# Tap and bias rows spread by TensorE, two whole filter transforms, wide FIR matmuls and DMA transposes in an SSM convolution with an MLP

## The chip, the cores and the metric

The kernel runs on one core of a Trainium2 chip. The metric is the device time of one execution in microseconds. The engines are PE (TensorE, matmuls, with weight loads shown apart as PEld), DVE (VectorE), ACT (ScalarE), POOL (GpSimd) and SP (SyncE, which issues DMAs). Data lies in SBUF; PE writes to PSUM, and DVE or ACT move results from there ("eviction").

## The reference

Two layers of two parts each, on a sequence of 2048 rows with 512 channels, all in bf16:

```python
def _A_ref(q, k, v, shift_k, ssm_k, ssm_D):          # q is the normed x
    for t in range(4):
        k_shift = k_shift + k_pad[:, t:t + S, :] * shift_k[:, 3 - t]
    kv = k_shift * v
    y = irfft(rfft(kv padded to 2S) * rfft(ssm_k padded to 2S))[:S]   # long causal convolution
    y = y + kv * ssm_D
    return q * y

def _B_ref(x, w1, b1, w2, b2):                        # x is normed, and normed again inside
    h = _gelu(_layernorm(x) @ w1 + b1)                # 512 -> 1376
    return h @ w2 + b2                                # 1376 -> 512

x = A_q
for layer in (0, 1):
    x = x + _A_ref(_layernorm(x), A_k, A_v, A_shift_k, A_ssm_k, A_ssm_D)
    x = x + _B_ref(_layernorm(x), B_w1, B_b1, B_w2, B_b2)
```

The convolution's input `kv` and its filter don't depend on x, so its result is computed once and used by both layers.

## The kernel before

**Blocks.** The sequence is cut into four blocks of 512 rows, b = 0 to 3, and so is the filter. Each block of 512 rows is transformed with 1024-point tables, as matmuls. `forward` transforms a block: for two sets of frequencies c and for the even and odd rows it runs 4 matmuls of 512 columns into PSUM, evicts the result, and then adds and subtracts the even and odd halves on DVE (`tt`); that makes 16 matmuls and 4 evictions a block. `spectrum_h(m)` transposes filter block m on PE (16 transposes), evicts it and calls `forward`; the results are called H0 to H3. `shift(b)` is the four-tap filter on k (the FIR): 16 transposes, an eviction, 64 matmuls of 128 x 128 against diagonal matrices that hold the taps, and a product with v. `products(b)` multiplies spectra, the sums over earlier blocks being made by accumulating DMAs from POOL's queue. `wrap(m)` folds filter block m-1 into m. `inverse(b)` transforms back with 16 matmuls.

**The MLP.** `mlp(b, L)` works on one block in layer L: statistics (DVE, with the power of -1/2 on POOL), norms (ACT, `norm`), a product with the convolution's result and an add (DVE), statistics and norms again, 8 PE transposes and an eviction for each pair of 128-row tiles, then 44 matmuls with W1 (11 groups of 4; twice 44 of half the width where PARTS splits the block, as for block 3 in both layers), GELU on ACT with the bias of each group as a per-partition scalar, and 44 matmuls with W2 of 512 columns. The eight MLPs are (block, layer): (0,0), (1,0), (0,1), (2,0), (1,1), (3,0), (2,1), (3,1), about in this order on PE.

**The order of work.** All operations are recorded first, as numbered operations with what they read and write. Three tables then settle where they run: ORDER, one list of all operation numbers, gives each engine's program order; SIDE names those that run on the second of two possible engines; BANKS gives PSUM banks. `replay` goes through the list with assumed durations, `keep_busy` puts dummy matmuls (L913 before, L985 after) into long gaps of PE in that replay, and `sync` adds semaphore waits for what remains dependent. Every engine runs its list strictly in order, so an instruction that waits holds up those behind it. SP's list is the queue of loads, and of the stores.

**The start.** SP loads k's first block, the identity, the taps (pieces of four values, straight into 128 partitions) and the first filter block, in this order. DVE multiplies identity and taps into 16 diagonals in one operation (L570). The MLP bias comes later in the same queue, in two DMAs of two-byte pieces, and POOL casts it to f32 (L549).

**Lines.** L557 is `tt`; L563 and L564 are evictions by ACT and DVE; L575 is a transform matmul; L605 and L629 are the transposes of the filter and of k; L648 is the FIR; L657 is its product with v from PSUM; L738 is the power on POOL; L750 and L752 are statistics; L779 is a norm; L807 is the MLP's transposes; L824 and L843 are W1 and W2; L829 is GELU; L848 and L851 add W2's result to x.

Of the kernel before, what the change touches and what calls it, by code (L numbers as in the profile page):

```python
# [7 lines left out]
ALU = mybir.AluOpType  # L8
# [358 lines left out]
def _tables():  # L367

    t = np.arange(4)[:, None] + 4 * np.arange(128)[None, :]
    kk = np.arange(2)[:, None] + 2 * np.arange(128)[None, :]  # L370
    th = TWO_PI * t[:, :, None, None] * (kk + 0.5) / 1024
    F = np.stack([np.cos(th), -np.sin(th)], 3)
    return F.transpose(1, 0, 2, 3, 4).reshape(128, 2048), F.transpose(4, 2, 3, 0, 1).reshape(128, 2048) / 512


SIDE = [30, 204, 508, 590, 728, 750, 831, 912, 933]
BANKS = "020402242404224400262556463010456340262616542032024240042240042440066016553462243501654013266102613202040404062341663552015021261526103315215340424444026015654624643030521242141654360010665123404156021610322554431541243501601"
ORDER = [
# [44 lines left out]
U = 512  # L423


def bass_interleave_layers__ssm_conv_h3__mixer_channel_mlp__prompt_kernel(
# [120 lines left out]
    for p0, n, o, c in ((0, 128, 0, 10), (0, 96, 10, 1)):  # L547
        d, s = M(p0, n, M_B1 + o, [1, c]), A(p0, n, R_B1 + o // 10 * 16, [1, c])
        P.op(POOL, lambda e, d=d, s=s: e.tensor_copy(d, s), 300.0, reads=[s], writes=[d])  # L549
# [394 lines left out]
```

## Time and profile before

| | us |
|---|---|
| median of 3 runs | 245.52 (245.1 to 245.62) |
| the profiled execution | 244.91 |
| its span, first to last instruction | 243.1 |
| PE busy | 232.9 (96%) |
| DVE busy | 185.1 (76%) |
| ACT busy | 181.6 (75%) |
| POOL busy | 68.0 (28%) |

The profile is of one execution. A row of the timeline gives start, length, engine, line, operation, output and input, and the count of instructions merged into it; in brackets stands the idle time ahead of it and what ended it. The chain of waits follows the last instruction back from releaser to releaser. A busy PE is not PE at its peak, since matmuls are pipelined and their recorded lengths overlap: what a stream of matmuls costs is the distance from one to the next.

### The profile page before, as it was taken

Reading aid. Unit: us, or ns where it says so; the run is one execution under the profiler, and the core shown is the slowest. Engines: PE = TensorE matmul, PEld = TensorE weight load, DVE = VectorE, ACT = ScalarE, POOL = GpSimd, SP = SyncE. Lnnn points to the kernel's source line nnn. Section 1 sums busy time; section 2 is a strip of 40 time slices with the busy share of each in tenths; the row PEclk is TensorE's granted clock in tenths of the full one; section 3 lists DMA queues with packets and bytes.
Section 4 is the critical chain, followed back from the end, with each engine's and each line's share of the span. In section 5 each row is a group of like instructions: output and inputs, shape, how many; then the busy total and the mean of one; then the engine's idle time right before and its main releaser. Section 6 shows DMA issues by size and latency. Waiting matters only on the chain.

```text
span 243.1 us, 3962 instructions
## 1 busy us (share of the span) xinstructions
PE 232.9 (96%) x1551; PEld 131.9 (54%) x1574; DVE 185.1 (76%) x357; ACT 181.6 (75%) x279; POOL 68.0 (28%) x73
## 2 busy tenths in 40 slices
PE   8999996989999999999999999999999999999994
PEld 3756632647655684445444544544468654448841
DVE  1379999999999999999999999783977242574004
ACT  2358998999899589979799285579968657955730
POOL 0000134432572356753146315241310201120000
PEclk9999999999999999999999999999999999999999
DMA  6999916668794099990089989920002000002002
GB/s 189 392 377 220 391 52 238 105 242 162 142 158 62 0 173 173 175 174 3 0 162 185 172 215 226 207 47 3 1 0 89 0 0 3 0 0 86 3 0 86
DMA packets 14406, 29.85 MB, mean 123 GB/s; under 512 B 3026, under 2 KB 8500, under 8 KB 14260
## 3 DMA queue, kind: packets, MB, share of 16 engines
q0 software_dynamic: 5232, 15.21, 32.9%
q1 hardware_dynamic: 9156, 14.40, 17.2%
q8 instruction: 12, 0.20, 0.3%
q14 instruction: 6, 0.05, 0.1%
HBM read 12.30 MB, written 2.10 MB: 59 GB/s over the span
## 4 chain that ended last, share of the span: by engine, by line
PE 67%; DVE 22%; issue 5%; ACT 3%; POOL 2%; DVEq 0%; POOLq 0%
PE ps L824 28%; PE ps L843 26%; DVE ar L557 14%; PE ps L575 6%; DVE sm L750 4%; PE ps L913 3%; PE ps L807 2%; POOL sm L738 2%; ACT ar L779 1%; DVE ar L657 1%; ACT ar L563 1%; DVE ar L851 1%; PE ps L629 1%; PE ps L648 1%; DVE sm L752 1%
## 5 line engine op out<-in xcount | busy, mean ns | idle before, releaser
L557 DVE TENSOR_TENSOR ar<-ar 128x2048 bf16<-128x2048 bf16 (+2 forms) x125 | 115.1, 954 | 9.3 <-ACT ar L563 4.8
L824 PE MATMUL ps<-ar 128*128 128x256 bf16 (+3 forms) x479 | 80.2, 320 | 1.2 <-ACT ar L563 0.9
L563 ACT ACTIVATE ar<-ps 128x1024 bf16<-128x1024 f32 (+2 forms) x61 | 64.3, 1115 | 22.0 <-PE ps L575 10.3
L843 PE MATMUL ps<-ar 128*128 128x512 bf16 (+1 forms) x339 | 79.6, 379 | 0.7
L829 ACT ACTIVATE ar<-ps,sm 128x256 bf16<-128x256 f32 (+3 forms) x121 | 61.5, 572 | 16.5 <-PE ps L824 16.2
L738 POOL TENSOR_TENSOR sm<-sm 128x2 f32<-128x2 f32 x32 | 39.0, 1218 | 104.6 <-DVE sm L757 45.1
L824 PEld LDWEIGHTS ps<-ar 128*128 128x128 bf16 (+1 forms) x484 | 47.7, 100 | 32.3 <-ACT ar L563 1.8
L779 ACT ACTIVATE ar<-ar,sm 128x512 bf16<-128x512 bf16 x64 | 48.4, 808 | 13.3 <-DVE sm L739 13.1
L843 PEld LDWEIGHTS ps<-ar 128*128 128x128 bf16 (+1 forms) x352 | 34.1, 98 | 37.0 <-ACT ar L829 1.2
L575 PE MATMUL ps<-ar 128*128 128x512 bf16 x187 | 44.4, 380 | 3.5 <-ACT ar L563 2.7
L620 POOL DMA_DIRECT2D ar<-ar x30 | 27.5, 931 | 44.8 <-DVE ar L557 25.3
L750 DVE BATCH_NORM_STATS2 sm<-ar 128x6 f32<-128x512 bf16 x48 | 32.5, 687 | 0.4
L575 PEld LDWEIGHTS ps<-ar 128*128 128x128 bf16 x192 | 17.2, 98 | 27.2 <-ACT ar L563 7.7
L851 DVE TENSOR_TENSOR ar<-ps,ar 128x512 bf16<-128x512 f32 x16 | 10.9, 686 | 16.6 <-PE ps L843 16.5
L848 DVE SCALAR_TENSOR_TENSOR ar<-ps,ar 128x512 bf16<-128x512 f32 x16 | 11.0, 685 | 8.4 <-PE ps L843 8.3
L648 PE MATMUL ps<-ar 128*128 128x128 bf16 x256 | 15.6, 219 | 0.3 <-ACT ar L563 0.2
L648 PEld LDWEIGHTS ps<-ar 128*128 128x128 bf16 x256 | 14.7, 98 | 1.8 <-ACT ar L563 0.7
L564 DVE COPY ar<-ps 128x1024 bf16<-128x1024 bf16 (+1 forms) x9 | 7.3, 808 | 7.7 <-PE ps L605 3.9
L771 ACT ACTIVATE ar<-ar,sm 128x512 bf16<-128x512 bf16 x16 | 11.5, 717 | 0.1
L913 PE MATMUL ps<-ar 128*128 128x512 bf16 x34 | 9.4, 428 | 1.0 <-DVE ar L523 1.0
L807 PE MATMUL ps<-ar 128*128 128x128 bf16 x128 | 9.5, 219 | 0.5 <-ACT ar L779 0.4
L807 PEld LDWEIGHTS ps<-ar 128*128 128x128 bf16 x128 | 8.1, 98 | 3.0 <-ACT ar L779 0.9
(27 smaller groups left out, 53.5 us busy)
## 6 DMA issues: line engine op xcount, KB each, us to landing
ar<-ar POOLq DMA_DIRECT2D x24, 512.0 KB, 4.9
ar<-in_A_k_dram SPq DMA_DIRECT2D x4, 512.0 KB, 5.6
ar<-in_A_ssm_k_dram SPq DMA_DIRECT2D x4, 512.0 KB, 8.0
ar<-in_A_v_dram SPq DMA_DIRECT2D x4, 512.0 KB, 5.8
ar<-in_A_q_dram SPq DMA_DIRECT2D x4, 512.0 KB, 7.0
ar<-ar POOLq DMA_DIRECT2D x6, 256.0 KB, 4.6
out_dram<-ar SPq DMA_DIRECT2D x3, 512.0 KB, 2.6
ar<-in_B_w_dram SPq DMA_DIRECT2D x1, 1376.0 KB, 7.1
```

Source lines behind the costliest of these rows:

```text
L557: return P.op(DVE, lambda e: e.tensor_tensor(o, a, b, op), 66.0 + 0.52 * n, reads=[a, b], writes=[o])
L563: return e.activation(dst, src(), AF.Copy)
L575: r = e.matmul(Q(tl, 0, 128, ri * 512, [1, 512]), w, m, start=a, stop=z)
L620: P.op(POOL, lambda e: e.dma_start(dst, src, accum_op=ALU.add), 880.0, reads=[src, dst], writes=[dst], dma=True, nbytes=nb)
L648: r = e.matmul(Q(tl, 0, 128, q, [1, 128]), w, m, start=j == 0, stop=j == 3)
L738: P.op(POOL, lambda e: e.tensor_tensor(r, v, hf, ALU.pow), 1100.0, reads=[v, hf], writes=[r])
L750: P.op(DVE, lambda e, st=st, x=x: e.bn_stats(st, x), 600.0, reads=[x], writes=[st])
L779: P.op(ACT, lambda e: e.activation(o, x, AF.Identity, bias=m, scale=r), 705.0, reads=[x, m, r], writes=[o])
L807: r = e.transpose(QB(tl, 0, 128, 256 * j + 128 * a, [1, 128]), src[4 * a + j], IDN)
L824: r = e.matmul(Q(tl, 0, rows, 0, [1, n]), w, m, start=dk == 0, stop=dk == 3)
L829: P.op(ACT, lambda e, dst=dst, tl=tl, rows=rows, bias=bias, n=n: e.activation(dst, Q(tl, 0, rows, 0, [1, n]), AF.Gelu_apprx_tanh, bias=bia ...
L843: r = e.matmul(Q(tl, 0, 128, 0, [1, 512]), ins[fc][0], ins[fc][1], start=fc == 0, stop=fc == 10)
```

## The change

1. *Taps.* The taps are loaded as one row of 2048 values into one partition, by ACT's queue, and so is the identity behind it; both are issued ahead of ACT's table load for GELU, which stands later in ACT's list now. 16 matmuls with one row and one column (`columns`, L562 after) spread the row over 128 partitions, an eviction follows, and the diagonals are made in two halves.
2. *Bias.* It is loaded as one row, spread by 11 such matmuls, and copied from PSUM by DVE. POOL's two casts go.
3. *First block of k.* Its transposes and their eviction are cut into two halves.
4. *FIR.* A block's FIR is 28 matmuls of 512, 384, 256 or 128 columns in place of 64 of 128; they multiply as many columns in all. PSUM now holds channels by half, so the product with v is strided.
5. *Filter blocks 1 and 2* are transformed whole by `direct`: 32 matmuls in place of 16, with negated tables for half of them (made once by `negate`), and no adding and subtracting on DVE. The transform of filter block 2 stands ahead of the first MLP in the recording.
6. *Frequencies.* The second set of frequencies is 768, 770, ... in place of 1, 3, ...; `wrap` is the same for both sets with it. For blocks 2 and 3 `products` adds and subtracts the two sets (4 more DVE operations of 1024 elements a block), and `inverse` takes 8 matmuls in place of 16.
7. *MLP inputs of (3,0), (2,1) and (3,1).* The 8 PE transposes and the eviction for each pair of tiles become two DMA transposes, issued by SP.
8. ORDER, SIDE and BANKS are new throughout. The assumed duration of the power on POOL is 690 in place of 1100.

```diff
-    kk = np.arange(2)[:, None] + 2 * np.arange(128)[None, :]
+    kk = 768 * np.arange(2)[:, None] + 2 * np.arange(128)[None, :]
...
+    row, src = A(0, 1, R_ACC + 512, [1, 2048]), dr(A_shift_k, 0, [0, 1], [1, 2048])
+    P.op(ACT, lambda e: e.dma_start(row, src), 500.0, writes=[row], dma=True, nbytes=4096)
+    ident, isrc = A(0, 128, R_ID, [1, 128]), bass.AP(t_id, 0, [[128, 128], [1, 128]])
+    P.op(ACT, lambda e: e.dma_start(ident.bitcast(mybir.dt.uint16), isrc), 500.0, writes=[ident], dma=True, nbytes=32768)
...
-    tload(t_id, 128, 0, R_ID, 128)
-    dma(A(0, 128, R_S, [4, 4], [1, 4]), dr(A_shift_k, 0, [4, 128], [512, 4], [1, 4]), 300000)
...
-    dma(A(0, 128, R_B1, [1, 10]), dr(B_b1, 0, [1, 128], [128, 10]), 2560)
-    dma(A(0, 96, R_B1 + 16, [1, 1]), dr(B_b1, 1280, [1, 96], [1, 1]), 192)
+    dma(A(0, 1, R_HT[0], [1, 1376]), dr(B_b1, 0, [0, 1], [1, 1376]), 2752)
...
+    def columns(rows):
+        tl = Tile(P, 1)
+        ins = [(q, len(r.ap) and r.ap[-1][1], r) for q, r in enumerate(rows)]
+        def f(e, ins=ins, tl=tl):
+            for q, n, r in ins:
+                o = e.matmul(Q(tl, 0, n, q, [1, 1]), r, one, start=True, stop=True)
+            return o
...
+    def direct(src, dst):
+        for c in range(2):
+            for z in range(2):
+                tl = Tile(P, 2)
+                ins = []
+                for ri in range(2):
+                    for i in range(4):
+                        w = A(0, 128, R_HT[0] + 4096 + ((i // 2 * 2 + c) * 2 + ri) * 128, [1, 128]) if z and i % 2 else fw(i, c, ri)
+                        ins.append((ri, i == 0, i == 3, w, A(0, 128, src + i * U, [1, U])))
+                freq(tl, ins)
+                copy(A(0, 128, dst + 2 * c * 1024 + z * 1024, [1, 1024]), tl, lambda tl=tl: Q(tl, 0, 128, 0, [1, 1024]), 1024)
...
+        if m in (1, 2):
+            return direct(o, R_H[m])
...
-                i = 2 * h + z
-                for c in range(4):
-                    for j in range(4):
-                        ins.append((z * 512 + c * 128, j, A(0, 128, kt + (c * 4 + (i - j) % 4) * 129 + (i >= j), [1, 128]),
-                                    A(0, 128, R_DG + (c * 4 + j) * 128, [1, 128])))
+                c = 2 * h + z
+                for m in (0, 1, 2, 3, -1, -2, -3):
+                    ins.append((z * 512 + max(m, 0) * 128, A(0, 128, kt + (c * 4 + m % 4) * 129 + (m >= 0), [1, 128]),
+                                A(0, 128, R_DG + (c * 4 + max(-m, 0)) * 128, [1, 128 * (4 - abs(m))]), m == 0, m == -3, 128 * (4 - abs(m))))
...
-            if c:
-                accumulate(re, pi, 410000)
-                tt(im, im, pr, ALU.subtract, 1024)
-            else:
-                tt(re, re, pi, ALU.subtract, 1024)
-                accumulate(im, pr, 410000)
+            tt(re, re, pi, ALU.subtract, 1024)
+            accumulate(im, pr, 410000)
...
+        if b in (2, 3):
+            for o in range(2):
+                u = A(0, 128, R_ACC + 512 + 1024 * o, [2048, 2], [1, 512])
+                v = A(0, 128, R_ACC + 4608 + 3072 * o, [-2048 if o else 2048, 2], [1, 512])
+                for z in range(2):
+                    tt(A(0, 128, R_ACC + 4096 * z + 1024 * o, [2048, 2], [1, 512]), u, v, ALU.subtract if z else ALU.add, 1024)
...
+            if (b, L) in ((2, 1), (3, 0), (3, 1)):
+                for a in range(2):
+                    zs, dst = A(0, 128, z + a * 512, [1, 512]), A(0, 128, xt + (i + a) * 128, [512, 4], [1, 128])
+                    P.op(SP, lambda e, zs=zs, dst=dst: e.dma_start_transpose(dst, zs), 1300.0, reads=[zs], writes=[dst], dma=True, nbytes=1 << 17)
+                continue
...
-ORDER = [
-    0, 1, 2, 3, 28, 4, 5, 6, 7, 8, 9, 10, 11, 44, 12, 13, 27, 45, 14, 15, 16, 17, 18, 46, 19, 20, 21, 22, 29, 97, 48, 202,
+ORDER = [
+    0, 2, 4, 5, 29, 22, 1, 6, 7, 8, 9, 10, 11, 24, 12, 13, 50, 25, 14, 48, 27, 15, 49, 16, 51, 17, 26, 54, 18, 19, 20, 21,
```

How instructions stand now is shown at three places. In the rows `ps` is PSUM, `ar` the one SBUF tensor, the shape is that of the output, and x is how many stand in a row. First the start of PE's list; before:

```order
L913 MATMUL ps<-ar 128x512 x15
L629 MATMUL ps<-ar 128x128 x16
L913 MATMUL ps<-ar 128x512 x9
L648 MATMUL ps<-ar 128x128 x32
L605 MATMUL ps<-ar 128x128 x16
L648 MATMUL ps<-ar 128x128 x32
L575 MATMUL ps<-ar 128x512 x12
```

And after, where L985 are the dummies, L562 the tap columns, L669 the transposes of k, L697 the FIR, L642 the transposes of the filter:

```order
L985 MATMUL ps<-ar 128x512 x11
L562 MATMUL ps<-ar 128x1 x16
L669 MATMUL ps<-ar 128x128 x16
L985 MATMUL ps<-ar 128x512 x5
L697 MATMUL ps<-ar 128x512
L697 MATMUL ps<-ar 128x384
L697 MATMUL ps<-ar 128x256
L697 MATMUL ps<-ar 128x128
L697 MATMUL ps<-ar 128x384
L697 MATMUL ps<-ar 128x256
L697 MATMUL ps<-ar 128x128
```

The tap columns stand ahead of k's transposes, and fewer dummies stand on both sides of them; the seven FIR rows are one quarter of a block.

Second, PE's list from the inverse of block 3 to the first W1 matmuls of MLP (3,0), which are the first with 256 columns; before (L575 with 8 is half of the inverse, L807 the transposes):

```order
L575 MATMUL ps<-ar 128x512 x8
L824 MATMUL ps<-ar 128x512 x4
L575 MATMUL ps<-ar 128x512 x8
L843 MATMUL ps<-ar 128x512 x30
L807 MATMUL ps<-ar 128x128 x8
L843 MATMUL ps<-ar 128x512 x7
L824 MATMUL ps<-ar 128x256 x8
```

And after (L590 is a transform matmul, L891 W1, L910 W2):

```order
L590 MATMUL ps<-ar 128x512 x4
L891 MATMUL ps<-ar 128x512 x8
L590 MATMUL ps<-ar 128x512 x4
L910 MATMUL ps<-ar 128x512 x44
L891 MATMUL ps<-ar 128x256 x40
L910 MATMUL ps<-ar 128x512 x4
L891 MATMUL ps<-ar 96x256 x4
```

The inverse has half as many matmuls, no transposes stand in PE's list, and all 44 W2 matmuls of the MLP before stand between the inverse and W1.

Third, the end of SP's list; before:

```order
L495 DMA out_dram<-ar 128x2048
L495 DMA ar<-in_A_q_dram 128x2048
L495 DMA out_dram<-ar 128x2048 x2
L495 DMA out_dram<-ar 128x512 x4
```

And after (L866 is a DMA transpose):

```order
L496 DMA out_dram<-ar 128x2048
L496 DMA ar<-in_A_q_dram 128x2048
L866 DMA_TRANSPOSE ar<-ar 128x4x128 x10
L496 DMA out_dram<-ar 128x2048
L866 DMA_TRANSPOSE ar<-ar 128x4x128 x2
L496 DMA out_dram<-ar 128x2048
L496 DMA out_dram<-ar 128x512 x4
```

The first ten transposes are those of (3,0), (2,1) and the first pair of (3,1); the last two stand behind the store of block 1's result.

More of the change, by code (lines that the diff above doesn't have):

```diff
@@ L554, in bass_interleave_layers__ssm_conv_h3__mixer_channel_mlp__prompt_kernel @@
     IDN = A(0, 128, R_ID, [1, 128])
+    one = A(0, 1, R_ID, [1, 1])
+    def columns(rows):
[5 more added lines that the diff above has]
+            return o
+        P.op(PE, f, len(ins) * 64.0, reads=[r for q, n, r in ins] + [one], tile=tl)
+        return tl
     def tt(o, a, b, op, n):
@@ L565, in copy @@
         P.op(engs, f, {ACT: 70.0 + .833 * n, DVE: 75.0 + n * (.52 if fast else 1.04)}, writes=[dst], tile=tl)
-    dg = A(0, 128, R_DG, [128, 16], [1, 128])
-    i3, s3 = A(0, 128, R_ID, [0, 16], [1, 128]), A(0, 128, R_S, [1, 16], [0, 128])
-    P.op(DVE, lambda e: e.tensor_tensor(dg, i3, s3, ALU.mult), 2300.0, reads=[i3, s3], writes=[dg])
+    tl = columns([A(0, 1, R_ACC + 512 + c * 512 + j, [4, 128]) for c in range(4) for j in range(4)])
+    copy(A(0, 128, R_S, [1, 16]), tl, lambda tl=tl: Q(tl, 0, 128, 0, [1, 16]), 150, (ACT, DVE))
+    for z in range(2):
+        dg = A(0, 128, R_DG + 1024 * z, [128, 8], [1, 128])
+        i3, s3 = A(0, 128, R_ID, [0, 8], [1, 128]), A(0, 128, R_S + 8 * z, [1, 8], [0, 128])
+        P.op(DVE, lambda e, dg=dg, i3=i3, s3=s3: e.tensor_tensor(dg, i3, s3, ALU.mult), 1180.0, reads=[i3, s3], writes=[dg])
     def freq(tl, ins):
@@ L596, in forward, with negate @@
                 tt(A(0, 128, dst + z * 1024, [2048, 2], [1, 1024]), e, o, ALU.subtract if z else ALU.add, 2048)
+    negf = A(0, 128, R_HT[0] + 4096, [512, 2], [1, 512])
+    posf = A(0, 128, R_F + 512, [1024, 2], [1, 512])
+    def negate(e):
+        if e is nc.scalar:
+            return e.activation(negf, posf, AF.Copy, scale=-1.0)
+        return e.tensor_scalar(negf, posf, -1.0, None, ALU.mult)
+    P.op((ACT, DVE), negate, {ACT: 930.0, DVE: 360.0}, reads=[posf], writes=[negf])
+    def direct(src, dst):
[9 more added lines that the diff above has]
+                copy(A(0, 128, dst + 2 * c * 1024 + z * 1024, [1, 1024]), tl, lambda tl=tl: Q(tl, 0, 128, 0, [1, 1024]), 1024)
     def spectrum_h(m):
@@ L623, in shift, with f @@
         kt = R_KT[b % 2]
-        tl = Tile(P, 2)
-        ins = [(c, i, A(0, 128, KS(b) + i * U + c * 128, [1, 128])) for c in range(4) for i in range(4)]
-        def f(e, ins=ins, tl=tl):
-            for c, i, src in ins:
-                r = e.transpose(QB(tl, 0, 128, c * U + i * 128, [1, 128]), src, IDN)
-            return r
-        P.op(PE, f, 16 * 60.0, reads=[x[2] for x in ins] + [IDN], tile=tl)
-        copy(A(0, 128, kt + 1, [129, 16], [1, 128]), tl, lambda tl=tl: QB(tl, 0, 128, 0, [128, 16], [1, 128]), 2048, (ACT, DVE), True)
+        for z in range(2) if b == 0 else ():
+            tl = Tile(P, 1)
+            ins = [(c, i, A(0, 128, KS(b) + i * U + (2 * z + c) * 128, [1, 128])) for c in range(2) for i in range(4)]
+            def f(e, ins=ins, tl=tl):
+                for c, i, src in ins:
+                    r = e.transpose(QB(tl, 0, 128, c * U + i * 128, [1, 128]), src, IDN)
+                return r
+            P.op(PE, f, 8 * 60.0, reads=[x[2] for x in ins] + [IDN], tile=tl)
+            copy(A(0, 128, kt + 8 * 129 * z + 1, [129, 8], [1, 128]), tl, lambda tl=tl: QB(tl, 0, 128, 0, [128, 8], [1, 128]), 1024, (ACT, DVE), True)
+        if b:
+            tl = Tile(P, 2)
+            ins = [(c, i, A(0, 128, KS(b) + i * U + c * 128, [1, 128])) for c in range(4) for i in range(4)]
+            def f(e, ins=ins, tl=tl):
+                for c, i, src in ins:
+                    r = e.transpose(QB(tl, 0, 128, c * U + i * 128, [1, 128]), src, IDN)
+                return r
+            P.op(PE, f, 16 * 60.0, reads=[x[2] for x in ins] + [IDN], tile=tl)
+            copy(A(0, 128, kt + 1, [129, 16], [1, 128]), tl, lambda tl=tl: QB(tl, 0, 128, 0, [128, 16], [1, 128]), 2048, (ACT, DVE), True)
         if b:
@@ L737, in finish @@
         r, nm = M(0, 128, M_RS + 2 * k, [1, 2]), M(0, 128, M_NM + 2 * k, [1, 2])
-        P.op(POOL, lambda e: e.tensor_tensor(r, v, hf, ALU.pow), 1100.0, reads=[v, hf], writes=[r])
+        P.op(POOL, lambda e: e.tensor_tensor(r, v, hf, ALU.pow), 690.0, reads=[v, hf], writes=[r])
         small(lambda e: e.scalar_tensor_tensor(nm, mn, neg, r, ALU.mult, ALU.mult), [mn, r], nm)
@@ L873, in conv @@
         inverse(b)
+    tl = columns([A(0, 1, R_HT[0] + fc * 128, [1, 128 if fc < 10 else 96]) for fc in range(11)])
+    for n, o, c in ((128, 0, 10), (96, 10, 1)):
+        d = M(0, n, M_B1 + o, [1, c])
+        P.op(DVE, lambda e, d=d, n=n, o=o, c=c, tl=tl: e.tensor_copy(d, Q(tl, 0, n, o, [1, c])), 150.0, writes=[d], tile=tl)
     tag("H0")
@@ L879, in bass_interleave_layers__ssm_conv_h3__mixer_channel_mlp__prompt_kernel @@
     spectrum_h(1)
+    tag("H2")
+    spectrum_h(2)
     tag("KP")
@@ L888, in bass_interleave_layers__ssm_conv_h3__mixer_channel_mlp__prompt_kernel @@
     load_v(2)
-    tag("H2")
-    spectrum_h(2)
     tag("H3")
```

41 lines of the change are left out of this document (25 added, 16 removed), and 81 rows, old and new, of the table ORDER.

## The prediction

> **What bounds the kernel now.** I read the page, then the chain of waits, then busy time by stage, and then each engine's timeline at the places where the stages meet.
>
> ```profile
> span 243.1 us, 3962 instructions
> PE 232.9 (96%) x1551; PEld 131.9 (54%) x1574; DVE 185.1 (76%) x357; ACT 181.6 (75%) x279; POOL 68.0 (28%) x73
> PEclk9999999999999999999999999999999999999999
> ...
> 8.74:91.11 82.37, 77.07 (x680) 48.98 (x689) 77.42 (x133) 68.45 (x86) 26.83 (x25) 1.00 0.71 188
> 91.11:240.07 148.96, 148.16 (x832) 79.35 (x846) 104.53 (x222) 110.02 (x192) 40.75 (x43) 1.00 0.38 79
> 240.07:243.10 3.03, 0.00 (x0) 0.00 (x0) 0.72 (x2) 0.00 (x0) 0.00 (x0) 0.95 0.37 130
> ```
>
> The last three rows are stages (length, then busy PE, weight loads, DVE, ACT, POOL, clock, DMA). From 91.11 to 240.07 us PE is busy 148.16 of 148.96 us: a PE instruction removed there is worth its own time. The 3.03 us behind it are the last adds and the output DMA. The first stage needs the chain:
>
> ```profile
> 37.69 6.35 DVE ar L557 x7
> 44.04 0.60 DVE sm L750
> 44.65 1.12 DVE ar L557
> 45.77 0.09 DVE sm L752
> 45.86 0.58 DVE ar L557
> ...
> 86.59 0.17 DVE sm L739
> ...
> 91.11 9.44 PE ps L824 x43
> ...
> 107.25 2.59 PE ps L843 x12
> ...
> 199.08 0.45 PE ps L807 x8
> ```
>
> Up to 86.76 us nearly every piece is DVE; then come the norms of block 1's first MLP on ACT, its transposes, and at 91.11 us its first W1 matmul. So DVE sets the first stage and PE the second. PE has slack in the first, though it looks busy there: its records overlap, and the spacing is 2.59/12 = 0.216 us for a matmul of 512 columns, and 0.45/8 = 0.056 us for a transpose. DVE spacings are 1.12 us for 2048 elements and 0.58 for 1024.
>
> **The opening.** Times are start and length.
>
> ```profile
> 0.98 4.80 PE L913 MATMUL ps<-ar 128*128 128x512 bf16 x15 [0.98 <-DVE ar L523]
> 5.62 1.06 PE L629 MATMUL ps<-ar 128*128 128x128 bf16 x16
> 6.52 2.11 PE L913 MATMUL ps<-ar 128*128 128x512 bf16 x9
> 8.74 1.95 PE L648 MATMUL ps<-ar 128*128 128x128 bf16 x32
> ...
> 6.72 1.88 ACT L563 ACTIVATE ar<-ps 128x2048 bf16<-128x2048 bf16 x1 [4.71 <-PE ps L629]
> ...
> 5.39 2.29 DVE L570 TENSOR_TENSOR ar<-ar 128x2048 bf16<-128x2048 bf16 x1 [4.47 <-DMA ar<-in_A_shift_k_dram]
> 19.42 1.28 DVE L750 BATCH_NORM_STATS2 sm<-ar 128x6 f32<-128x512 bf16 x2
> ```
>
> PE runs dummies (L913) until k's first block lands at 5.6 us. The FIR starts at 8.74, behind a transposed copy that takes ACT 1.88 us and ends at 8.60. Halved and shared by ACT and DVE, the copy ends about 0.9 us earlier. The diagonals end at 7.68 now. Afterwards the tap row and the identity must land, 16 one-column matmuls run, and DVE builds the diagonals in halves of 1.15 us with its half of the copy between them. If the columns are done by 5.5 us, the first half is there by 6.8. I take the FIR start at 8.0 us; the ends are 7.6 (copy alone) and 9.0 (taps land as late as k).
>
> **PE in the first stage.** The order of instructions gives the counts from the first FIR matmul to that W1 matmul. Before: 256 FIR matmuls at 1.95/32 = 0.061 (15.6), 144 transform matmuls (31.1), 144 transposes (8.1), 88 W1 of 256 columns at half of 0.216 (9.5), 44 W2 (9.5): 73.8 us in 82.37, so 8.5 us are waits, or dummies put into waits. After: the same FIR columns in 112 wider matmuls, at 0.216 per 512 (13.8); 176 transform matmuls (38.0), since the whole transforms of filter blocks 1 and 2 take 32 instead of 16 each; the same transposes, W1 and W2; 11 bias columns at 0.06 (0.7). That is 79.6 us. From 8.0, PE alone could be done at 87.6.
>
> The Trainium skill says otherwise of the spacing ("TensorE: Matmul & The Clock Gate", Back-to-back issue gap): about 81 ns at 128 columns and 131 at 512 in a real stream. By that the FIR would cost 20.7 us now and the 32 extra matmuls 4.2. The trace disagrees, with 61 and 216 ns, and the rows decide.
>
> **DVE in the first stage.** From its first statistics at 19.42 to 86.76 DVE is never idle for long: 67.3 us. The order has in the same stretch one operation of 2048 elements fewer (28 for 29), three of 1024 fewer, and one add from PSUM fewer, against two tiny copies. The four combining operations of filter blocks 1 and 2 are gone (4 x 1.12 = 4.5), and others have moved up in their place. Net: 1.12 + 1.75 + 0.6 - 0.2 = 3.3 us less. But three additions of 1024 and half a copy now stand ahead of the statistics (1.75 + 0.6 more, part of it in idle time), while the FIR comes 0.7 earlier, so I let the stretch begin 1.1 later, at 20.5. DVE is done at 84.5, and with the same 4.35 us behind it the stage would end at 88.9.
>
> Two limits, 87.6 and 88.9, now lie 1.3 us apart where they were 8.5 apart, so waits of one engine no longer vanish in the other's slack. I add 1.1 us and take 90.0, 1.1 less than now.
>
> **The second stage.** Blocks 2 and 3 invert with 8 matmuls instead of 16: 16 x 0.216 = 3.46 us. Three MLPs lose 48 transposes: 48 x 0.056 = 2.7. Both lie on the chain, so 148.96 becomes 142.8. The price is on DVE: eight operations of 1024, 8 x 0.58 = 4.6, half per block.
>
> ```profile
> 100.00:120.00 20.00, 19.89 (x104) 9.54 (x105) 19.65 (x44) 16.85 (x23) 6.92 (x8) 1.00 0.43 81
> 120.00:140.00 20.00, 19.89 (x105) 9.62 (x105) 19.62 (x34) 15.03 (x27) 10.10 (x11) 1.00 0.83 158
> 140.00:160.00 20.00, 19.89 (x104) 9.77 (x105) 18.02 (x40) 12.57 (x19) 6.30 (x8) 1.00 0.98 211
> ```
>
> DVE has 0.35 us of room in 20 until 140, so block 2's 2.3 us have no cover there but DVE's lead of 86.76 - 84.5 = 2.3 us from the first stage. It just pays. Block 3's lie in 140 to 160, which has 2 us free. I book nothing.
>
> **The DMA transposes.** The sharp place is block 3's first MLP, whose input hangs on its own inverse.
>
> ```profile
> 166.14 1.89 PE L575 MATMUL ps<-ar 128*128 128x512 bf16 x8
> ...
> 176.94 0.61 PE L807 MATMUL ps<-ar 128*128 128x128 bf16 x8
> ...
> ar<-ar POOLq DMA_DIRECT2D x24, 512.0 KB, 4.9
> ...
> out_dram<-ar SPq DMA_DIRECT2D x4, 128.0 KB, 1.7
> ```
>
> Now the first half of the inverse ends at about 167.9, and the normed rows are ready for transposing at 176.9: 9.0 us of copy, statistics and norms. Afterwards PE has 8 W1, 4 inverse and 44 W2 matmuls between the two: 56 x 0.216 = 12.1 us. That leaves 3.1 us for two DMA transposes, the second issued 0.8 us behind the first (one norm). No row shows a transpose. The nearest are 1.7 us (same size and queue, to HBM) and 4.9 (four times the size, SBUF to SBUF, with adding). I take t = 2.5, nearer to the row of its size. One after another they end 2t - 0.8 = 4.2 us behind the norm, 1.1 too late; at t = 1.7 there is no wait. SP issues them in order and each waits for its norm; behind them wait only later transposes and outputs, with more room: the last MLP's W1 stands 44 + 44 matmuls behind the one ahead of it. I book 1.5 us for all three MLPs.
>
> The Trainium skill's "DMA: Bandwidth & Descriptors" (Latency and other measured facts; Anatomy of one DMA) gives 261 GB/s for strided transposes and about 2 us fixed; my estimate from it is 2.5 us each, and the sum would be the same. No run here shows it yet.
>
> **Costed at nothing.** The bias load in two-byte pieces:
>
> ```profile
> 17.29 3.58 SPq L495 DMA_DIRECT2D ar<-in_B_b_dram  x1
> ...
> ar<-in_B_b_dram SPq DMA_DIRECT2D x1, 2.5 KB, 8.0
> ```
>
> It goes, and W1 and the fourth filter block are issued some 4 us earlier; neither was waited for. The second table load on ACT (1.28 us) and the two DMA issues there lie in ACT's slack, 68.45 busy of 82.37. If ACT paces PE at that place, up to 1.3 us comes back.
>
> **Sum.** 90.0 + 142.8 + 1.5 + 3.03 = 237.3 us of span, 5.8 less than 243.1. The profiled execution took 244.91, so 239.1; the median of the runs shown is 0.6 above that execution: 239.7 us.
>
> **Rivals.**
> *The first stage keeps its waits.*
>
> ```profile
> 35.61 0.81 PE L913 MATMUL ps<-ar 128*128 128x512 bf16 x3
> 36.57 1.90 PE L575 MATMUL ps<-ar 128*128 128x512 bf16 x8
> 38.31 1.67 PE L913 MATMUL ps<-ar 128*128 128x512 bf16 x7
> 41.91 2.59 PE L575 MATMUL ps<-ar 128*128 128x512 bf16 x11 [1.92 <-ACT ar L563]
> ```
>
> PE's 8.5 us may not be slack but the shape of the dependences (eviction, then DVE, then the next transform); nearly half of it stands in these rows, ten dummies and a wait on an eviction. Then the whole transforms don't fill it: 8.0 + 79.6 + 8.5 = 96.1, 6.1 more than I take, 245.8 us. For it: PE waits there on evictions, which the change doesn't shorten. Against: the added matmuls need no DVE result, and DVE's list is shorter.
> *The transposes are slow.* If t is 4.9 like the SBUF row, the first pair is 2 x 4.9 - 3.9 = 5.9 late, and the second, needed 40 W1 of 256 and 4 W2 later (5.2 us), adds 9.8 - 5.2 = 4.6: 10.5 in place of 1.5, so 248.7 us. It decides against the change from about t = 4.1, where the wait is 7.3. A wait of over 3 us may also slow the clock: the first 15 dummies took 4.80 us, 0.32 each against 0.216 later, and the change has dummies only at the start (16 for 34). The Trainium skill ("TensorE: Matmul & The Clock Gate", HAM oscillation) says that PE falls to half clock after some 3.4 us idle; the opening agrees with a slow start, while no wait here is long enough to test it.
> *Both fit.* No pile-up and no transpose wait: 88.9 + 142.8 + 3.03 = 234.7, so 237.1 us.
>
> **How the numbers follow.** My forecast (238 to 242) has 0.50, both fit 0.15, the waits that stay 0.20 (kept in part it still ends below before: 0.11 faster, 0.05 same, 0.04 slower), slow transposes 0.15, slower. Same means within 0.2% (0.5 us), about what a measurement can tell. Faster: 0.50 + 0.15 + 0.11 = 0.76; same 0.05; slower 0.04 + 0.15 = 0.19. The range runs from 236.0 (FIR at 7.6, both fit) to 246.5, past the waits that stay and short of the slow transposes.
>
> **What would show it.** First W1 matmul of block 1 near 90 us; from there to PE's end 142.8 us plus little; 28 FIR matmuls a block in about 3.5 us; inverse of blocks 2 and 3 in 8 matmuls; transposes landing in 2 to 3 us, with a PE wait of about 1 us ahead of block 3's first W1. I am wrong if the first stage ends past 93, if transposes take over 4 us, or if DVE, 4.6 us heavier, runs late for block 2's next MLP between 110 and 140.

## The result, and the profile after

The changed kernel takes 242.49 us (median of 8 runs, 240.87 to 244.64), the kernel before beside it 245.47 (8 runs). The ratio is 0.9866, interval 0.9835 to 0.9898: 1.3% faster. The profiled execution took 242.87 us. The runs differ by the granted clock: at a mean clock of 1.0 they took 240.87 to 242.3, at 0.993 they took 242.67 to 243.15, and the longest had 0.986; that one is left out of the ratio. Where the clock's fall comes from is below.

The page of the changed kernel begins:

```profile
span 241.1 us, 3649 instructions
PE 231.5 (96%) x1382; PEld 127.0 (53%) x1407; DVE 183.2 (76%) x360; ACT 180.5 (75%) x281; POOL 58.6 (24%) x71
...
PEclk9999999997999999999999999999999999999999
```

PE is as busy as before by its share, but the clock has a dent, in the tenth of 40 slices (54 to 60 us). The same stages as in the prediction, cut at the first FIR matmul, at block 1's first W1 matmul and at PE's end (length, then busy PE, weight loads, DVE, ACT, POOL, clock, DMA):

```profile
8.61:94.39 85.78, 81.19 (x564) 48.52 (x576) 77.36 (x134) 70.01 (x87) 23.07 (x25) 0.98 0.73 190
94.39:237.98 143.59, 142.74 (x773) 75.05 (x784) 103.13 (x223) 108.01 (x192) 34.53 (x39) 1.00 0.42 88
237.98:241.10 3.12, 0.00 (x1) 0.00 (x0) 0.73 (x2) 0.00 (x0) 0.00 (x0) 1.00 0.24 84
```

The second stage went from 148.96 to 143.59 us, a gain of 5.4. The first ended at 91.11 and ends at 94.39 now: 3.3 us of that gain are given back there. The chain of waits shows the place (start, length, what):

```profile
35.25 4.66 DMA ar<-ar
...
40.21 9.61 DMA ar<-ar
...
49.91 1.23 DVE ar L568
...
56.19 1.14 DVE ar L568
57.33 0.12 DVE ar L685
...
57.78 2.23 PE ps L697 x8
```

The first DMA is a copy of filter block 1 that is kept for a later `wrap` (L713, 1 MB), and W1, which is `wrap` of filter block 1, is issued behind it; the second is one of W1's two accumulating DMAs of 256 KB, which takes 9.61 us. DVE waits for it (2.39 us by its timeline) and works through its list; at 57.33 it comes to the 0.12 us copy of S2's tap column (L685), and only then can PE begin S2's FIR (S2 is `shift` of block 2). What that does to PE, by its timeline, and to the clock, by windows of 2 us:

```profile
53.85 1.06 PE L679 MATMUL ps<-ar 128*128 128x128 bf16 x16
57.78 3.19 PE L697 MATMUL ps<-ar 128*128 128x384 bf16 x13 [2.87 <-DVE ar L685]
```

```profile
56.00:58.00 2.00, 0.22 (x1) 0.27 (x3) 2.00 (x5) 1.77 (x3) 0.57 (x1) 0.91 0.99 186
58.00:60.00 2.00, 2.00 (x9) 1.13 (x8) 2.00 (x4) 2.00 (x2) 0.86 (x1) 0.50 1.03 197
60.00:62.00 2.00, 2.00 (x19) 1.56 (x17) 2.00 (x3) 0.85 (x2) 0.82 (x1) 0.73 0.97 184
```

PE stands for 2.87 us, its clock falls to 0.50, and 13 FIR matmuls take 3.19 us that take 1.69 at full clock. SP's timeline, and the DMAs that POOL issues from 30 to 62 us (count, size of each, median us to landing), show what ran beside the accumulates:

```profile
37.36 0.35 SPq L496 DMA_DIRECT2D ar<-in_A_v_dram  x1
37.75 1.23 SPq L496 DMA_DIRECT2D ar<-in_A_k_dram  x1
...
40.26 0.67 SPq L496 DMA_DIRECT2D ar<-in_A_q_dram  x1
```

```profile
ar<-ar POOLq DMA_DIRECT2D x3, 256.0 KB, 9.6
```

Two of these three are W1's (9.61 and 11.3 us); the third comes later and takes 4.0.

The first of five loads (two are left out here), v3 (block 3 of v), had waited 19.1 us for PE's last matmul of K1, block 1's transform, which reads the room that v3 is loaded into. k2, q1, v2 and q2 stand behind it in SP's list, so all five go out together, 2.5 MB, just as the accumulates start. In the kernel before, k2 and q1 went out earlier, by its timeline of SP:

```profile
23.03 1.46 SPq L495 DMA_DIRECT2D ar<-in_A_k_dram  x1
24.53 0.45 SPq L495 DMA_DIRECT2D ar<-in_A_q_dram  x1
```

The rest went much as the code says. In the second stage W1 of block 3's first MLP (L891) follows the W2 matmuls without a wait, and the DMA transposes land in 2.5 us (first PE's timeline, then the issues of the whole page):

```profile
171.05 9.68 PE L910 MATMUL ps<-ar 128*128 128x512 bf16 x43
180.57 4.53 PE L891 MATMUL ps<-ar 128*128 128x256 bf16 x40
```

```profile
ar<-ar SPq DMA_TRANSPOSE x12, 2.5
```

### The profile page after: what moved, and what is told of

It reads as the page before. It is cut to its first block, busy times and chain, and to the rows that moved or that the text cites. A ratio compares the mean times of both kernels' runs of the same rounds, so it can differ in the third digit from the quotient of the medians.

```text
span 241.1 us, 3649 instructions
## 1 busy us (share of the span) xinstructions
PE 231.5 (96%) x1382; PEld 127.0 (53%) x1407; DVE 183.2 (76%) x360; ACT 180.5 (75%) x281; POOL 58.6 (24%) x71
## 4 chain that ended last, share of the span: by engine, by line
PE 68%; DVE 15%; ACT 7%; DMA 6%; issue 2%; POOL 0%; DVEq 0%; POOLq 0%
PE ps L910 28%; PE ps L891 27%; DVE ar L568 9%; DMA ar<-ar 6%; PE ps L590 5%; PE ps L697 4%; ACT ar L896 2%; ACT ar L841 2%; DVE sm L812 2%; PE ps L985 2%; ACT ar L574 2%; PE ps L874 2%; DVE ar L575 1%; ACT ar L833 1%; DVE ar L709 1%
## 5 line engine op out<-in xcount | busy, mean ns | idle before, releaser
L568 DVE TENSOR_TENSOR ar<-ar 128x1024 bf16<-128x1024 bf16 (+2 forms) x129 | 115.9, 927 | 8.5 <-ACT ar L841 3.8
L891 PE MATMUL ps<-ar 128*128 128x256 bf16 (+3 forms) x479 | 79.7, 320 | 0.4
L910 PE MATMUL ps<-ar 128*128 128x512 bf16 (+1 forms) x343 | 79.4, 379 | 0.5
L574 ACT ACTIVATE ar<-ps 128x1024 bf16<-128x1024 f32 (+3 forms) x61 | 62.8, 1090 | 14.2 <-PE ps L590 7.4
L896 ACT ACTIVATE ar<-ps,sm 128x256 bf16<-128x256 f32 (+3 forms) x121 | 60.8, 569 | 9.9 <-PE ps L891 9.8
L891 PEld LDWEIGHTS ps<-ar 128*128 128x128 bf16 (+1 forms) x484 | 47.8, 100 | 31.3 <-ACT ar L896 1.2
L800 POOL TENSOR_TENSOR sm<-sm 128x2 f32<-128x2 f32 x32 | 29.6, 924 | 104.1 <-DVE sm L819 39.3
L910 PEld LDWEIGHTS ps<-ar 128*128 128x128 bf16 (+1 forms) x352 | 34.1, 98 | 38.8 <-ACT ar L896 0.7
L590 PE MATMUL ps<-ar 128*128 128x512 bf16 x201 | 47.0, 379 | 1.4 <-DVE sm L945 0.7
L590 PEld LDWEIGHTS ps<-ar 128*128 128x128 bf16 x208 | 19.7, 98 | 23.6 <-DVE ar L709 1.4
L697 PE MATMUL ps<-ar 128*128 128x256 bf16 (+3 forms) x108 | 15.9, 303 | 3.1 <-DVE ar L685 2.9
L697 PEld LDWEIGHTS ps<-ar 128*128 128x128 bf16 x112 | 10.2, 104 | 8.5 <-DVE ar L685 2.8
L801 DVE SCALAR_TENSOR_TENSOR sm<-sm 128x2 f32<-128x2 f32 x32 | 4.7, 152 | 4.9 <-POOL sm L800 4.8
L814 DVE BATCH_NORM_AGGREGATE sm<-sm 128x2 f32<-128x6 f32 x48 | 8.1, 173 | 0.2
L575 DVE COPY ar<-ps 128x1024 bf16<-128x1024 bf16 (+1 forms) x5 | 4.5, 896 | 4.7 <-PE ps L679 2.9
L985 PE MATMUL ps<-ar 128*128 128x512 bf16 x16 | 6.1, 551 | 1.0 <-DVE ar L527 1.0
```

The lines of the kernel that those rows point to most:

```text
L568: return P.op(DVE, lambda e: e.tensor_tensor(o, a, b, op), 66.0 + 0.52 * n, reads=[a, b], writes=[o])
L574: return e.activation(dst, src(), AF.Copy)
L590: r = e.matmul(Q(tl, 0, 128, ri * 512, [1, 512]), w, m, start=a, stop=z)
L697: r = e.matmul(Q(tl, 0, 128, q, [1, n]), w, d, start=a, stop=o)
L800: P.op(POOL, lambda e: e.tensor_tensor(r, v, hf, ALU.pow), 690.0, reads=[v, hf], writes=[r])
L891: r = e.matmul(Q(tl, 0, rows, 0, [1, n]), w, m, start=dk == 0, stop=dk == 3)
```

## The experiments

Two theories. *Late sum*: the first stage lost its time because W1's accumulates ran beside the late loads; DVE stood, handed on late, PE stood, and the clock fell. *Full stage*: the whole transforms' 6.9 us of extra PE work fill the first stage, and the waits only change their place. In three kernels the loads stay late: in those of "The clock by itself" and "The tap column's copy earlier", and in the first of the two by halves. In the others they are moved as in the first experiment ("The same traffic" says how it differs), and the times are read against its time. PE's dummies at the opening stay what they are unless said, and `keep_busy` is held to the first 20 us of its replay wherever an edit would bring in more. The kernels ran on three chips, and the kernel before took 245.49 to 245.8 us beside them, so a difference of 0.3 us between two experiments tells nothing. Where an edit adds or takes away lines, the line numbers shift by one or a few.

### The loads moved

```diff
 L496 DMA ar<-in_A_ssm_k_dram 128x4x512
-L496 DMA ar<-in_A_v_dram 128x2048
 L496 DMA ar<-in_A_k_dram 128x2048
 L496 DMA ar<-in_A_q_dram 128x2048
 L496 DMA ar<-in_A_v_dram 128x2048
 L496 DMA ar<-in_A_q_dram 128x2048
+L496 DMA ar<-in_A_v_dram 128x2048
 L496 DMA ar<-in_A_k_dram 128x2048
```

> The loads of k2, q1, v2 and q2 stand ahead of v3's in SyncE's list, so that they no longer stand behind its wait of 19.1 us; nothing else moves. Late-sum theory (the first stage lost its time because W1's accumulating DMAs ran together with these loads, so that VectorE stood 2.39 us and handed S2's filter its tap column late): k2 and q1 are issued before 27 us, W1's accumulates land within 6 us where they took up to 11.3, VectorE's wait of 2.39 us is gone, TensorE's wait of 2.87 us ahead of S2's FIR falls under 1 us, the granted clock stays 1.00 there; first stage ends at about 90.5 to 91.5 where it ended at 94.39, time 238.5 to 239.6 us. Full-stage theory (the 6.9 us of extra TensorE work of the whole transforms fill the first stage and the waits only change place): the stage ends within 1 us of 94.4, time 241.5 to 243 us.

Measured: 239.09 us (238.77 to 239.2); ratio to the kernel before 0.9728, interval 0.9707 to 0.975, clear of the changed kernel's. SP's timeline, POOL's accumulates as above, and PE's timeline:

```profile
17.85 1.45 SPq L496 DMA_DIRECT2D ar<-in_A_k_dram  x1
...
22.10 0.43 SPq L496 DMA_DIRECT2D ar<-in_A_q_dram  x1
37.36 0.33 SPq L496 DMA_DIRECT2D ar<-in_A_v_dram  x1
```

```profile
ar<-ar POOLq DMA_DIRECT2D x3, 256.0 KB, 4.0
```

```profile
55.24 1.69 PE L697 MATMUL ps<-ar 128*128 128x384 bf16 x13 [0.39 <-DVE ar L685]
...
90.60 9.66 PE L891 MATMUL ps<-ar 128*128 128x512 bf16 x43
```

The accumulates take 4.0 us in the median (W1's two 4.3), DVE's wait is gone, PE's is 0.39, the FIR runs at full clock, and the first stage ends at 90.60: 3.8 us earlier. The wait is 2.5 us shorter and the FIR 1.5, and 0.2 of that is lost again by the stage's end. Late sum, as expected; full stage is out as the cause of the loss. This kernel is faster than both others, by the moves in one list.

### The same traffic, needed by nobody

Was it the traffic, or did something need k2, q1, v2 or q2 sooner? Here k2 and q1 are loaded early, as above, and once more at the old place into room that nobody reads; v2 and q2 stay behind v3.

```diff
+    for d, t in ((A(0, 128, R_HT[0] + 2048, [1, 4 * U]), A_k), (A(0, 128, R_XT + 2048, [1, 4 * U]), A_q)):
+        dma(d, dr(t, 0, [4 * 512, 128], [1, 4 * U]), 1 << 19)
```

> k2 and q1 are loaded early, as with the moved loads, so that nothing of the computation waits for the late ones; but behind v3's load, at 37.4 us, stand two further loads of 512 KB (k2 and q1 once more, into room that nobody reads), then v2 and q2, so that the DMA engines have the changed kernel's 2.5 MB of loads at the same place as there. If it is the traffic beside the keeping copy and W1's accumulates that makes these late: accumulates of 7 to 11 us, VectorE waits 1.5 to 2.5 us for them again, TensorE 2 to 3 us ahead of S2's FIR, first stage 93 to 94.4, time 240.8 to 243 us. If the loads had mattered because something needed k2, q1, v2 or q2 sooner: as with the moved loads, 239.0 to 239.4 us.

Measured: 242.61 us (240.71 to 242.95), the changed kernel's time again. POOL's accumulates, PE's timeline (L698 is the FIR, L892 W1) and the clock:

```profile
ar<-ar POOLq DMA_DIRECT2D x3, 256.0 KB, 9.4
```

```profile
57.25 3.45 PE L698 MATMUL ps<-ar 128*128 128x512 bf16 x14 [2.39 <-DVE ar L686]
...
94.14 6.21 PE L892 MATMUL ps<-ar 128*128 128x512 bf16 x28
```

```profile
58.00:60.00 2.00, 2.00 (x11) 1.23 (x9) 2.00 (x4) 2.00 (x2) 0.86 (x1) 0.50 0.88 164
```

Everything is back (W1's two accumulates take 10.3 us in the median), so the traffic alone makes the sum late. (The profile puts DVE's 2.13 us here down to PE; but PE's stream up to 54 us lies where it lay with the moved loads, 53.80 against 53.79 for the next transposes, and there the same DVE operation began 2.2 us earlier. What is new is the DMA.) The Trainium skill ("DMA: Bandwidth & Descriptors", Issuing engines are not separate DMA queues) says that DMAs of all issuing engines run on the same 16 engines and interleave; 9.4 us against 4.0 for POOL's accumulates beside SP's loads agrees.

### The clock by itself

```diff
+    at = [o.pos for o in q if o.tag == "S2"][1]
+    for i in range(11):
...
+        d.fn = lambda e: e.matmul(idle, zero, zeros, start=True, stop=True)
...
+        q.insert(at, d)
```

> 11 matmuls of zeros (0.22 us each at full clock, 2.4 us together) stand in TensorE's list ahead of S2's FIR, where it waited 2.87 us. Late-sum theory with the clock's fall as a part of its own: the wait keeps its place (the FIR begins at 57.8 +- 0.4), but the clock stays at 1.00 and the FIR's 13 matmuls take about 1.75 us where they took 3.19; time 240.8 to 241.3 us in every run, where the kernel without them had 240.87 to 244.64. If the clock falls whatever TensorE does there: 3.2 us again, 242.5 us.

Measured: 241.49 us (240.83 to 242.19), all five runs at clock 1.0. PE's timeline (L992 are the new dummies) and the clock:

```profile
54.19 2.54 PE L992 MATMUL ps<-ar 128*128 128x512 bf16 x11
57.15 1.69 PE L697 MATMUL ps<-ar 128*128 128x384 bf16 x13 [0.42 <-DVE ar L685]
```

```profile
58.00:60.00 2.00, 2.00 (x23) 1.55 (x22) 2.00 (x3) 2.00 (x3) 0.86 (x1) 1.00 0.88 166
```

The FIR begins 0.6 us earlier than in the changed kernel, since the opening of this execution was 0.5 us earlier (its first FIR matmul at 8.11), so the wait keeps its place; the FIR runs in 1.69 us. So the clock's fall hangs on PE's idle time, and it costs this FIR 1.5 us. The medians differ by 1.0, less, as not every run of the changed kernel has the fall. The times reach past the 240.8 to 241.3 that were expected.

### The tap column's copy earlier

The copy L685 stands ahead of the addition that waits for the accumulate; the loads stay late.

```diff
+L685 COPY ar<-ar 128x16
 L568 TENSOR_TENSOR ar<-ar 128x2048
...
-L685 COPY ar<-ar 128x16
```

> VectorE's 0.19 us copy of S2's tap column, for which TensorE waited 2.87 us, stands ahead of the addition that waits for W1's accumulate (57.25 before, 49.9 or earlier now); the accumulates stay late. Late-sum theory: the FIR begins at 54.9 to 55.3, right behind the filter transposes, at full clock (1.75 us for 13 matmuls); then TensorE waits for ScalarE's normalizations, which VectorE hands on late still: 0 to 1.5 us there; time 239.5 to 241.3 us. If the wait only moves to the transposes behind it, in full: within 0.5 of 241.1 us at full clock, 242.5 where the clock falls. Full-stage theory: 242 +- 0.5.

Measured: 243.72 us (241.3 to 244.55). PE's timeline:

```profile
56.62 1.69 PE L697 MATMUL ps<-ar 128*128 128x384 bf16 x13
59.71 0.62 PE L874 MATMUL ps<-ar 128*128 128x128 bf16 x8 [1.41 <-ACT ar L841]
61.47 3.47 PE L697 MATMUL ps<-ar 128*128 128x512 bf16 x14 [1.14 <-ACT ar L574]
```

The FIR begins right behind the transposes, but PE then waits for a norm and an eviction on ACT, 2.55 us in two pieces, and the clock falls there. The wait moves, nearly in full (2.55 for 2.87), as the second reading expected: its two runs at clock 1.0 and 0.999 took 241.3 and 241.73 us, and the copy is only where DVE's lateness comes through. The median is 1.2 us above the 242.5 expected with a fallen clock, and why isn't shown. This execution also began its first FIR matmul 1.7 us later than the others, of which the last section tells.

### Filter blocks 1 and 2 by halves again

```diff
-        if m in (1, 2):
-            return direct(o, R_H[m])
-        forward(o, R_H[m], (R_TMP, R_HT[0], R_EO[0], R_EO[0])[m], m > 0)
+        forward(o, R_H[m], (R_TMP, R_TMP, R_HT[0], R_EO[0])[m], m > 0)
```

First with the loads late:

> Filter blocks 1 and 2 transformed by halves again, as in the kernel before: 32 matmuls of 0.216 us less on TensorE (6.9 us), four 128x2048 additions of 1.2 us more on VectorE (4.8 us). Full-stage theory: TensorE's work sets the first stage, so it ends up to 6 us earlier, 237 to 240 us. Late-sum theory: VectorE sets when S2's FIR can begin, so it begins later, at 59 to 62, with a longer TensorE wait ahead of it; time 242.5 to 246 us.

Measured: 248.76 us (248.12 to 250.41), 2.8 above the range of the late sum; the FIR at 60.97 behind a wait of 3.10 us. Then with the loads moved:

> The moved loads, with filter blocks 1 and 2 transformed by halves as in the kernel before: 32 matmuls of 0.216 us less on TensorE, four 128x2048 additions of 1.2 us more on VectorE. VectorE's list is full from 38.6 to 61 us with the moved loads, so if VectorE sets when S2's FIR begins, it begins 3.5 to 5 us later than 55.24 with a TensorE wait of 3 us or more; first stage 94 to 97, time 242.5 to 246 us. If TensorE's work sets the first stage: 236 to 238.5 us.

Measured: 246.28 us (244.96 to 247.59). PE's timeline (L591 is a transform matmul, L696 the FIR, L890 W1), and the clock behind its two longest waits:

```profile
40.57 4.45 PE L591 MATMUL ps<-ar 128*128 128x512 bf16 x12 [3.87 <-DVE ar L569]
...
58.00 1.92 PE L696 MATMUL ps<-ar 128*128 128x512 bf16 x14 [0.16 <-DVE ar L684]
...
65.63 0.61 PE L890 MATMUL ps<-ar 128*128 128x256 bf16 x4 [2.65 <-ACT ar L575]
...
96.71 3.62 PE L890 MATMUL ps<-ar 128*128 128x512 bf16 x16
```

```profile
42.00:44.00 2.00, 2.00 (x6) 0.76 (x5) 1.97 (x3) 1.19 (x3) 1.14 (x2) 0.50 0.00 0
66.00:68.00 2.00, 2.00 (x21) 1.72 (x19) 2.00 (x6) 1.95 (x5) 0.88 (x1) 1.00 0.82 122
```

With 6.9 us less work for PE and 4.8 more for DVE, the first stage ends at 96.71 in place of 90.60, so PE's work doesn't set it. PE's waits are for DVE (3.87 us) and for ACT's evictions (2.65), but not where they were expected: S2's FIR begins 2.8 us later than with the moved loads, and its own wait is 0.16. The median is 0.3 us above the range. Some of the 6.1 us is the clock, whose mean is 0.979 to 0.993 in these runs: the 12 matmuls behind the first wait take 4.45 us, about 1.7 more than at 0.216 each. In this order the whole transforms are worth 7.2 us in the median. But the order was made for them, and no dummies fill the new waits here; what halves cost in an order of their own was not tried.

### The second stage's terms

PE transposes in place of DMA transposes, and 16 matmuls for the inverse in place of 8, each on top of the moved loads:

```diff
-            if (b, L) in ((2, 1), (3, 0), (3, 1)):
+            if (b, L) in ():
```

> On top of the moved loads (239.09 us), the last three MLP inputs are transposed by TensorE again: 48 transposes in six groups, each with an eviction of about 0.7 us on VectorE, and no transposing DMAs. By the prediction's term (48 transposes taken from TensorE were worth 2.7 us, and the DMAs that took their place cost TensorE nothing): 241.6 to 242.0 us. If the transposing DMAs cost a wait of 1.5 us that they had been booked with: 240.0 to 240.6 us.

Measured: 242.62 us (242.36 to 243.25), 3.5 more, above both ranges. PE's transposes (L874) in the second stage, by windows, with the moved loads and here:

```profile
90.60:238.00 147.40, 3.51 (x48) 3.02 (x48) 1.00 0.41 87
```

```profile
90.60:238.00 147.40, 7.18 (x96) 6.12 (x96) 1.00 0.35 75
```

The 48 transposes add 3.67 us by their records, which overlap their neighbours by a little (all of PE is busy 2.9 longer); two PE waits on ACT of 0.47 and 0.23 us are new.

```diff
-        for cs in () if b in (2, 3) else ((0,), (1,)) if b == 0 else ((0, 1),):
+        for cs in ((0,), (1,)) if b == 0 else ((0, 1),):
```

with the eight additions of `products` left out as well.

> On top of the moved loads, blocks 2 and 3 are inverted with 16 matmuls each again in place of 8, without the four additions each that made 8 possible. By the prediction's term (16 matmuls of 0.216 us less, VectorE's 8 additions of 0.58 us hidden): 242.3 to 242.7 us. If VectorE's additions had lain on the path, half of it comes back: 239.8 to 241 us.

Measured: 243.14 us (242.69 to 243.89), 4.05 more, also above both ranges. PE's transform matmuls are 3.24 us longer, and one new wait stands in its timeline:

```profile
157.12 0.62 PE L874 MATMUL ps<-ar 128*128 128x128 bf16 x8 [1.07 <-ACT ar L841]
```

DVE's additions cost nothing there; both edits measured somewhat more than their matmuls.

### FIR with narrow matmuls, and the table load

```diff
-                for m in (0, 1, 2, 3, -1, -2, -3):
+                for i in range(4):
+                    for j in range(4):
```

> On top of the moved loads, the FIR with 32 matmuls of 128 columns to a half block in place of 14 of up to 512, with the new taps and layouts left as they are; 1.95 us of TensorE a half in the kernel before, 1.74 to 1.91 in the changed one. If TensorE's work sets the time everywhere: 8 halves of 0.04 to 0.21 us, 239.4 to 240.8 us. If only VectorE's chain sets the first stage, where six of the halves lie: 239.0 to 239.6 us.

Measured: 239.55 us (239.23 to 239.76), 0.46 more, and the first stage ends at 91.38 in place of 90.60. Both ranges hold 239.55, so it doesn't tell the two apart; the wide matmuls are worth half a microsecond or so.

```diff
 L525 DMA ar<-tab_id 128x128
-L574 ACT_TABLE_LOAD
+L528 ACT_TABLE_LOAD
...
-L528 ACT_TABLE_LOAD
```

> On top of the moved loads, the table for GELU is loaded first on ScalarE, as in the kernel before, so that one load of 1.28 us at 30.65 us is gone from ScalarE's list, ahead of the last evictions of filter block 1 that the keeping copy and W1 wait for. If ScalarE's evictions there set when VectorE may begin W1's additions (38.6 us) and VectorE sets when S2's FIR begins, the first stage ends 0.8 to 1.3 us earlier: 237.8 to 238.3 us. If TensorE's work sets the first stage once the loads are moved: 238.9 to 239.3 us.

Measured: 238.89 us (238.83 to 238.92), ratio 0.973 as with the moved loads alone. ACT's timeline, where the load stood:

```profile
32.19 1.02 ACT L574 ACTIVATE ar<-ps 128x1024 bf16<-128x1024 f32 x1 [0.64 <-PE ps L590]
33.91 4.69 ACT L574 ACTIVATE ar<-ps 128x1024 bf16<-128x1024 f32 x5 [0.70 <-PE ps L590]
```

0.64 and 0.70 us of waiting for PE have taken the place of the 1.28 us. PE paces ACT there, and the load is free.

### Three small moves together

```diff
+L525 DMA ar<-tab_id 128x128
 L523 DMA ar<-in_A_shift_k_dram 1x2048
-L525 DMA ar<-tab_id 128x128
```

and the copy L685 and the table load moved as above; one dummy less stands at each of the two places of the opening.

> The moved loads, and three small moves: the identity's load ahead of the shift row's on ScalarE's queue (it landed at 5.8 us and TensorE's first real work waited for it), the copy of S2's tap column ahead of the addition that waits for W1's accumulate (0.39 us of TensorE wait left there), the GELU table first. If the opening and VectorE's list still set the first stage: the FIR begins at 8.1 to 8.3 where it began at 8.61, and 0.4 is saved at S2's: 238.2 to 238.5 us. If the shift row then lands last and TensorE's own work sets the rest: 238.9 to 239.3 us.

Measured: 238.68 us (238.26 to 239.23), ratio 0.9724, interval 0.9701 to 0.9746. PE's timeline:

```profile
7.54 1.92 PE L697 MATMUL ps<-ar 128*128 128x512 bf16 x14 [0.27 <-DVE ar L575]
...
89.93 9.66 PE L891 MATMUL ps<-ar 128*128 128x512 bf16 x44
```

The FIR begins 1.07 us earlier, the first stage ends 0.67 earlier, and the 0.4 us in the median lie within what the two intervals leave open. The time lies between the two ranges, so it doesn't tell the readings apart. The version to keep is the one with the moved loads; these moves may add a little.

## Why the prediction was right or wrong

The forecast of 239.7 us was 2.8 below the median, on the right side of the kernel before and inside the range, but only half of the forecast gain came (3.0 of 5.8 us), and by a sum in which the first stage failed: it ended past 93 us, which the prediction had named as a sign of being wrong. Against the predicted span of 237.3, the measured 241.1 is 3.8 more: first stage +4.4, second -0.7, tail +0.1.

- **The opening** (FIR at 8.0, ends 7.6 and 9.0) came at 8.61. The tap columns began at 5.79 us, where I had let them be done by 5.5, and they stand ahead of k's transposes; with the identity loaded ahead of the tap row, and one dummy less at each place, the FIR begins at 7.54 in the one execution that was profiled.
- **The first stage** (limits 87.6 and 88.9, 1.1 us added, 90.0 taken) ended at 94.39. The term that failed is the 1.1 us for "waits of one engine" in "the other's slack": it had no DMA in it. I had looked at SP's list for the bias, W1's weights and the fourth filter block, but not at the five loads behind them, whose order had changed so that one with a long wait stood first. Without that, the stage ends at 90.60, 0.6 past what I took. That this is so near is in part luck: DVE's stretch, which I let begin at 20.5, begins with its first statistics at 22.5, 0.6 of it from the later FIR; its length is 63.4 us with the moved loads where I had 64.0, so it is done at 85.9 in place of 84.5, and the 1.1 us that I had added for waits cover most of that.
- **DVE sets the first stage, PE has slack in it**: the halves (96.71) fit it, in an order not made for them, though not for all of the stage. Between 30 and 38 us PE paces ACT (the table load), and the narrow FIR makes the stage 0.8 us longer. The first rival's "against" held too: in this order the added matmuls cost less than the DVE work they save.
- **The second stage** (142.8, and 1.5 for the transposes) took 143.59. The two terms came to 6.2 us and the stage is 5.4 shorter; PE's idle time in it is 0.85 us where it was 0.80, so the 0.8 us lies in PE's spacing and not in waits, and I have no run that divides it. Undone one at a time, the inverse's term (3.46) measured 4.05 and the transposes' (2.7) measured 3.5; PE then also waits for ACT, and the two together are more than the stage gained, so they don't add up. DVE's 4.6 us more cost nothing, as booked.
- **The DMA transposes**: t = 2.5 was taken and 2.5 measured. The wait ahead of block 3's first W1 didn't come (no idle time stands at 180.57); of the 1.5 us booked, at most the 0.85 us by which PE's busy time falls short of the stage can have been spent.
- **Costed at nothing**: right for the bias's load and for the table load, whose "up to 1.3 us" did not come back. A PE wait of 0.70 us at 38.40 is put down to DVE's copy of the bias columns, which the prediction counted among "two tiny copies" on DVE alone; what it cost was not tried.
- **The rivals.** The measured stage end lies nearer to the first rival's 96.1 than to my 90.0, but not by its mechanism: the waits were not the shape of the dependences, since moving loads brings PE's wait of 2.87 us down to 0.39. Slow transposes didn't come, at 2.5 us each, nor did "both fit": with the loads moved the stage still ends 1.7 us past its 88.9. The clock's fall, which I had put behind a transpose wait of over 3 us, came in the first stage behind 2.87.

## What to carry to other kernels

When a change brings a new order, go down each DMA queue and ask of every transfer what it waits for and which transfers behind it are held up: the held load cost nothing by itself here, but the whole group, released at once, ran beside the DMA that was on the chain then, and made it late. A predicted limit of two engines holds only if no transfer that both hang on is slowed. And where a wait of some 2.5 us of TensorE can't be removed, dummies in it are worth trying: they kept the clock here in all five runs.

## What the runs showed of the hardware

An idle time of 2.39 us (same traffic) and of 2.87 us (changed kernel) was enough for the granted clock to fall to 0.50 within the next 2 us window; 1.92 us in the kernel before and 0.39 to 0.42 here were not. In the kernel by halves with the moved loads 3.87 us were enough, but 2.65 us were not: the clock reads 1.00 behind them. So the length of a wait doesn't settle it alone, and what else does isn't shown. Two waits of 1.41 and 1.14 us with 0.6 us of work between them did it too. The Trainium skill ("TensorE: Matmul & The Clock Gate", What's actually happening) speaks of an idle window of about 3.4 us; two of the waits here that lowered the clock are shorter, and the measurements decide. It does not fall every time: five of the six runs with the same traffic have a mean clock of 0.993 and took 242.54 to 242.95, the sixth has 1.0 and took 240.71.

The start of this program has a slow phase that the clock row doesn't show: it reads 1.00 while the first dummies are 0.44 us apart (4.87 us for 11), where a matmul of 512 columns later takes 0.216. PE's timeline in the changed kernel:

```profile
0.98 4.87 PE L985 MATMUL ps<-ar 128*128 128x512 bf16 x11 [0.98 <-DVE ar L527]
5.79 0.69 PE L562 MATMUL ps<-ar 1*128 1x1 bf16 x16
6.41 1.08 PE L669 MATMUL ps<-ar 128*128 128x128 bf16 x16
```

In the profiled execution of the kernel with the earlier copy, the identity came about 0.4 us later and PE stood 0.29 us for it:

```profile
6.15 0.69 PE L562 MATMUL ps<-ar 1*128 1x1 bf16 x16 [0.29 <-DMA ar<-tab_id]
6.78 1.89 PE L669 MATMUL ps<-ar 128*128 128x128 bf16 x16
```

The 16 transposes then took 1.89 us in place of 1.08, and the first FIR matmul came at 10.33 in place of 8.61. That one execution shows both things doesn't show that the 0.29 us caused the slow transposes; it was not tried by itself.
